# Building a causal filter's tap matrices with products on TensorE instead of a trip through DRAM

## The chip, the cores and the metric

The kernel runs on one core of a Trainium2 chip. The time is that of the whole device execution in microseconds, median of three runs. The engines are TensorE (PE in the profile; PEld is its weight load), VectorE (DVE), ScalarE (ACT), GpSimd (POOL) and SyncE (SP), which issues most of the transfers.

## What is computed

A causal filter of seven taps over the sequence, with softmax-normalised taps for each of 8 heads, and behind it two layers that expand 192 to 2048 and contract again, each with its own nonlinearity.

```python
# x: (2, 4096, 192), weight: (8, 7); a head has 24 of the 192 columns
w = exp(weight - max(weight)); w = w / (sum(w) + 1e-9)
out = einsum('hk,bskhg->bshg', w, windows_of_7(x_pad))     # filter over s
h = out.reshape(8192, 192) @ w_in                          # (192, 2048)
x = (h * clip(h + 3, 0, 6) / 6) @ w_out                    # layer 1
h = x @ w_in2
P = a[0] + a[1]*h + a[2]*h**2 + a[3]*h**3
Q = 1 + abs(b[0])*abs(h) + abs(b[1])*h**2
return (P / (Q + 1e-6)) @ w_out2                           # layer 2
```

## The kernel before

The 8192 rows are cut into 16 blocks of 512 (the last in two halves). Weights and activations are float32, split into a high and a low part; a product with weights runs three times (high by high, low by high, high by low). The contraction is laid out over 64 partitions, so that two products, one on partitions 0 to 63 and one on 64 to 127, run side by side on PE. The text calls these the two strands, L and H.

**The filter.** For each head a 64 x 128 matrix, `band`, holds the seven taps on shifted diagonals, and the filter is a product of `band` with the input rows. `band` has a copy on either half of the partitions. `xn` holds a block's rows as ten overlapping segments of 64 rows with 58 outputs each: five on partitions 0 to 63, five on 64 to 127. `conv0` and `conv1` (line 975 on) run the L and the H segments of four heads into one bank of PSUM; since both write the same bank, H starts only when L has ended (a *fence*, line 737: SP's queue is told by PE and tells PE). `conv_ev` copies the bank to SBUF (ACT, L1000), with a small copy on DVE (L998) that repeats the first heads at the row's end. `flip0`/`flip1` (L1012) then transpose with the reversing matrix `perm`, and ACT (L1024) and DVE (L1028) write the high and the low part into `X`, from which layer 1 reads. Blocks 0 and 1 are done ahead of all else and use the two banks `pre0` and `pre1`, which later are layer 1's accumulators; the first product of layer 1's contraction waits for block 1's last low part (`x1l2`).

**Making `band`.** `band_ops` (line 773) turns the taps, 7 numbers on 8 partitions, into the softmax with 19 small DVE instructions and transposes the result; `clear_line` and `store_line` write it into a zeroed DRAM line, `load_band` reads the line back with a stride of one element from partition to partition (twice, from SP and ACT), and `band_copy` copies it into `band` on ACT, POOL and DVE.

**Weights.** The 32 tiles of weights come as two words of 32 bits for each number and are put together on chip: `mag_w` on ACT (L869), `bound_w` on POOL or DVE (L874), three steps `bits_w` on DVE (L885, L888, L892), the high part on ACT (L903, L905), the low part on DVE or POOL (L912). A tile's raw words sit in one of four buffers; the next load into a buffer waits for the third step, which reads it last. PE cannot start a tile of the layer before its weights stand.

**What sets the order.** All instructions are listed with a due time and a guessed duration; `Issue.order` plays the list engine by engine and so fixes each engine's order; the numbers in `P` (offsets of due times, how far ahead an engine may look) steer it. Within an engine everything runs in that order. `warm` puts products of zeros on PE while it would idle at the start.

**The end.** The last block's contraction runs on exact words, and `P["GP"]` and `P["PATT"]` say which of its element-wise steps are done by POOL.

Of the kernel before, what the change touches and what calls it, by code (L numbers as in the profile page):

```python
# [27 lines left out]
 'CONV2': -0.275,  # L28
 'PAT': [1, 2],
 'PAT0': [1, 2],  # L30
 'PATT': [1, 2, 2, 2, 2, 2, 2, 0],
 'W1P': [-3.102, -2.87],
 'W2P': [6.57, 5.937],
 'WARM': 22,
 'TH': 0.001,
 'DUP': 2600,
 'WPART': {'c0': 0.1524, 'v0': 0.0728, 'vs': 0.0281, 'h0': 0.1693, 'l0': 0.2823},
 'HEAD': 32.39,
 'TAIL': 202.05,
 'D10': 3,  # L40
 'NEXT': -1.2,
# [11 lines left out]
          'dec': 65.4661,  # L53
          'conv': -4.205,
          'out': -156.0893,
          'x2': -18.5457,
          'fill': 999947.6802,
          'conv0': 26.2603},
 'OFF': {'mm1': -0.0531,
         'mm3': -0.6613,  # L60
         'mm2L': 1.4626,
         'mm2H': 2.4455,
         'mm4H': 1.0382,
         'mm4L': 0.3677,
         'u': -6.4348,
         'g': -32.961,
         'hi1': 4.7085,
         'lo1': -76.5356,
         'A': 3.8338,
         't1': 3.4597,  # L70
         'sq': 3.6846,
         'S': -175.4688,
         'q1': -55.5172,
         'q2': -103.6162,
         'q': -73.6019,
         't2': 3.5597,
         't3': -124.0539,
         'R': 4.9985,
         'RR': 5.6438,
         'w': -4.9954,  # L80
         'p2': -29.8916,
         'G': -111.7171,
         'hi2': 6.854,
         'lo2': 96.9644,
         'x2ah': -98.0086,
         'x2al': -54.7306,
         'x2mh': -3.2214,
         'x2ml': -14.6485,
         'x2mc': -67.402,
         'oa': -19.0233,  # L90
# [1254 lines left out]
```

## Time and profile before

| | us |
|---|---|
| three runs | 1232.18, 1232.56, 1233.94 |
| median | 1232.56 |
| profiled execution, its own time | 1232.17 |
| its span, first to last instruction | 1230.4 |
| PE busy | 1214.4 |
| DVE, ACT, POOL busy | 1137.3, 1140.7, 1107.9 |

The span is 1.8 us shorter than the execution that it belongs to. A busy PE is one with at least one product in flight; with two strands it can be busy and still do half of what it could. "Idle before" is an engine's idle time ahead of an instruction, and what stands behind the arrow released it.

### The profile page before, as it was taken

To read this page: it belongs to the slowest core of one execution; us is meant where nothing else is said; L and a number is where in the kernel's file an instruction comes from. 1 tells how busy PE (TensorE), PEld (TensorE's weight loads), DVE (VectorE), ACT (ScalarE), POOL (GpSimd) and SP (SyncE) were. 2 spreads that over 40 slices of the span, in tenths; PEclk is the share of its full clock that TensorE was granted. 3 is DMA by queue.
4 is the path that set the end of the run, shared out by engine and by line. 5 is a ranking of instruction groups with operands and counts; after the bars stand their busy time and mean duration, and the time that the engine had idled before them with its cause. 6 is when DMAs were issued, how large, how long until landed. Compare 5 with 4: busy or idle time off the path is not lost.

```text
span 1230.4 us, 31321 instructions
## 1 busy us (share of the span) xinstructions
PE 1214.4 (99%) x11334; PEld 1145.3 (93%) x11334; DVE 1137.3 (92%) x1807; ACT 1140.7 (93%) x2110; POOL 1107.9 (90%) x948
## 2 busy tenths in 40 slices
PE   9999999999999999999999999999999999999997
PEld 7788999899989999999999999999999999999997
DVE  6798999999999899899999999999999999999998
ACT  4677999999999999899999999999999999999996
POOL 3897998999989899898989989899899999999976
PEclk9999999999999999999999999999999999999999
DMA  6556003021030301203020020200202001011110
GB/s 161 142 161 157 18 2 71 2 52 21 1 71 2 72 1 25 48 2 72 1 52 21 11 63 2 54 19 14 59 14 50 10 15 44 14 28 27 52 28 14
DMA packets 75313, 51.46 MB, mean 42 GB/s; under 512 B 43290, under 2 KB 65174, under 8 KB 75158
## 3 DMA queue, kind: packets, MB, share of 16 engines
q1 hardware_dynamic: 74426, 48.89, 17.0%
q8 instruction: 89, 1.46, 0.5%
q10 hardware_dynamic: 732, 0.57, 0.2%
q14 instruction: 66, 0.54, 0.1%
HBM read 21.65 MB, written 7.87 MB: 24 GB/s over the span
## 4 chain that ended last, share of the span: by engine, by line
PE 84%; DVE 5%; ACT 5%; issue 2%; POOL 2%; DMA 1%; SPq 0%; DVEq 0%; ACTq 0%; POOLq 0%
PE acc L730 42%; PE bank L730 40%; PE warm L730 1%; DMA raw<-in_moe_w_out_dram 1%; DVE S L1192 1%; PE bank L1012 1%; DVE bank L1197 1%; DVE T L1165 1%; ACT T L1150 1%; ACT bank L1187 1%; ACT A L1146 1%; ACT A L1182 1%; DVE T L1205 1%; DVE T L1177 0%; POOL A L874 0%
## 5 line engine op out<-in xcount | busy, mean ns | idle before, releaser
L730 PE MATMUL bank<-X,Ih 64*128 64x512 f32 (+1 forms) x3264 | 905.6, 378 | 1.5 <-DVE T L1109 1.1
L730 PEld LDWEIGHTS bank<-X,Ih 64*128 64x128 f32 x3264 | 549.6, 184 | 20.6 <-DVE T L1109 1.9
L730 PE MATMUL bank<-X,Il 64*128 64x512 f32 (+1 forms) x1632 | 568.8, 375 | 0.0
L730 PE MATMUL acc<-g2h,O 64*128 64x512 f32 x1536 | 519.8, 392 | 2.1 <-SPq L737 2.0
L730 PE MATMUL acc<-g1h,O 64*128 64x512 f32 (+1 forms) x1536 | 493.7, 377 | 2.9 <-DVE X L1028 1.8
L730 PE MATMUL acc<-g2l,O 64*128 64x512 f32 x1024 | 397.0, 388 | 0.0
L730 PE MATMUL acc<-g1l,O 64*128 64x512 f32 (+1 forms) x1024 | 380.6, 374 | 0.3 <-POOL g1l L1117 0.3
L1171 POOL TENSOR_TENSOR S<-A,S 128x512 f32<-128x512 f32 x255 | 330.3, 1301 | 23.3 <-ACT A L1146 15.5
L1117 POOL TENSOR_TENSOR g1l<-u,g1h 128x512 fp32r<-128x512 f32 x240 | 311.9, 1300 | 31.1 <-ACT g1h L1113 25.6
L1220 POOL TENSOR_TENSOR g2l<-T,g2h 128x512 fp32r<-128x512 f32 x240 | 311.8, 1302 | 15.3 <-ACT g2h L1215 11.2
L730 PEld LDWEIGHTS bank<-X,Il 64*128 64x128 f32 x1632 | 290.8, 185 | 6.2
L730 PEld LDWEIGHTS acc<-g2h,O 64*128 64x128 f32 x1536 | 277.3, 184 | 11.7 <-SPq L737 4.8
L730 PEld LDWEIGHTS acc<-g1h,O 64*128 64x128 f32 x1536 | 276.3, 185 | 12.2 <-SPq L737 3.7
L1165 DVE SCALAR_TENSOR_TENSOR T<-T,coef,bank 128x512 f32<-128x512 f32 x256 | 190.2, 744 | 28.5 <-ACT A L1146 14.5
L1177 DVE SCALAR_TENSOR_TENSOR T<-T,coef,bank 128x512 f32<-128x512 f32 x256 | 190.4, 745 | 4.0 <-ACT A L1146 1.0
L730 PEld LDWEIGHTS acc<-g1l,O 64*128 64x128 f32 x1024 | 188.8, 184 | 5.1 <-POOL g1l L1117 0.7
L730 PEld LDWEIGHTS acc<-g2l,O 64*128 64x128 f32 x1024 | 188.5, 184 | 5.3
L1192 DVE SCALAR_TENSOR_TENSOR S<-S,bank 128x512 f32<-128x512 f32 x256 | 174.8, 683 | 13.5 <-ACT bank L1187 11.6
L1197 DVE SCALAR_TENSOR_TENSOR bank<-T,coef,bank 128x512 f32<-128x512 f32 x249 | 187.0, 751 | 0.0
L1150 ACT ACTIVATE T<-bank,coef 128x512 f32<-128x512 f32 x256 | 175.9, 688 | 10.2 <-PE bank L730 8.4
L1205 DVE SCALAR_TENSOR_TENSOR T<-S,bank 128x512 f32<-128x512 f32 x249 | 170.4, 684 | 4.1
L1109 DVE SCALAR_TENSOR_TENSOR u<-u,bank 128x512 f32<-128x512 f32 x240 | 163.5, 683 | 9.8 <-ACT u L1105 7.5
(104 smaller groups left out, 1797.5 us busy)
## 6 DMA issues: line engine op xcount, KB each, us to landing
X<-X SPq DMA_DIRECT2D x73, 256.0 KB, 3.3
raw<-in_moe_w_out_dram SPq DMA_DIRECT2D x16, 384.0 KB, 4.0
xn<-in_x_dram SPq DMA_DIRECT2D x27, 192.0 KB, 3.6
out_dram<-ov SPq DMA_DIRECT2D x60, 64.0 KB, 2.0
raw<-in_moe_w_in_dram SPq DMA_DIRECT2D x16, 192.0 KB, 3.7
raw<-in_moe_w_in_dram SPq DMA_DIRECT2D x16, 128.0 KB, 3.3
out_dram<-A SPq DMA_DIRECT2D x15, 128.0 KB, 2.0
saved<-A SPq DMA_DIRECT2D x8, 192.0 KB, 3.7
```

Of the source, the lines that this page charges most:

```text
L730: return nc.tensor.matmul(out=out, lhsT=lhsT, rhs=rhs, start=start, stop=stop, skip_group_check=True, **k)
L1012: i = nc.tensor.transpose(c[:, col:col + SPAN], src[:, 64 * part:64 * part + 128], rev[z])
L1109: stt(out=t, in0=t, scalar=1.0, in1=h1.pop((b, i)), op0=ALU.min, op1=ALU.mult)
L1117: nc.gpsimd.tensor_tensor(out=g1[b, i][1], in0=v1.pop((b, i)), in1=f32(g1[b, i][0]), op=ALU.subtract)
L1150: act(out=tile2(b, i, "T"), in_=h2[b, i], func=ACTF.Copy, scale=coef[:, 3:4])
L1165: stt(out=d["T"], in0=d["T"], scalar=coef[:, 2:3], in1=h2[b, i], op0=ALU.add, op1=ALU.mult)
L1171: (nc.gpsimd if k else nc.vector).tensor_tensor(out=d["S"], in0=d["A"], in1=d["S"], op=ALU.add if k == 1 else ALU.mult)
L1177: stt(out=d["T"], in0=d["T"], scalar=coef[:, 1:2], in1=h2[b, i], op0=ALU.add, op1=ALU.mult)
L1192: stt(out=d["S"], in0=d["S"], scalar=c1, in1=r2[b, i], op0=ALU.add, op1=ALU.mult)
L1197: stt(out=t if on_pool(b, i) else r2[b, i], in0=t, scalar=coef[:, 0:1], in1=r2[b, i], op0=ALU.add, op1=ALU.mult)
L1205: stt(out=d["T"], in0=d["S"], scalar=2.0, in1=k, op0=ALU.subtract, op1=ALU.mult)
L1220: nc.gpsimd.tensor_tensor(out=g2[b, i][1], in0=v2.pop((b, i))["T"], in1=f32(g2[b, i][0]), op=ALU.subtract)
```

## The change

**Taps.** `load_tap` reads the taps four times side by side (8 partitions x 28), and the same small DVE instructions run on them, without the transpose. A product with a small unit matrix (`band_rep`) spreads them over 128 partitions, one DVE product with a 0/1 mask (`band_diag`) keeps each head's tap where it belongs, and `band_mm` makes all bands in one PSUM bank with 16 float32 products of 32 columns, each of which is two passes on PE; behind each stands one pair of products of zeros. `band_ev` copies the bank into `band`, twice on ACT and twice on DVE. The 0/1 matrices are made at the start by POOL (one `iota`, four comparisons each for `step` and `eye`) and by DVE (`mask`). The DRAM line, its three transfers and `band_copy` are gone.

**Block 0.** Its L and H segments go into separate banks (`convz`): L into `pre0` and `pre1`, H into two ordinary banks, with no fence. `conv_ez` copies L on ACT, H on DVE, and the wrapped heads on DVE for each half.

**Order.** `P` has new numbers throughout. Fewer products of zeros stand at the start (5 rounds instead of 22). The loads of the first four weight tiles no longer wait for named events (`GATE`), the low part of the first weight tile moves from DVE to POOL (`LO0`), the convolution of block 2 is due earlier (`CONV2`), and in the last half block one `q` moves from DVE to POOL (`PATT`) and one product less runs on POOL (`GP`).

```diff
- 'CONV2': -0.275,
+ 'CONV2': -5.103,
- 'WARM': 22,
+ 'WARM': 5,
- 'PATT': [1, 2, 2, 2, 2, 2, 2, 0],
+ 'PATT': [1, 2, 2, 2, 2, 2, 2, 2],
- 'GATE': [2, 1, 2, 0],
+ 'GATE': [0, 0, 1, 0],
- 'LO0': [3],
+ 'LO0': [0, 3],
...
+        for hf in range(2 * (b == 0)):
+            for y in range(2):
+                k = ("pre", hf) if not y else ("bank", ("conv", hf))
+                at(t + hf * step, "c.trc", "LH"[y], 896, "convz", *(() if y else (4 + hf,)), hf, y, ...)
+                at(t + hf * step, "c.cv", "AV"[y], (451, 515)[y], "conv_ez", hf, y, ...)
...
-    at(-62, None, "S", 300, "store_line", ...)
-        at(-60 + 0.1 * z, None, "SA"[z], 480, "load_band", z, ...)
+    at(-64, None, "L", 300, "band_rep", r=[("line", 0), ("eye", 0)], w=[pb])
+    at(-63, None, "V", 90, "band_diag", r=[pb, ("mask", 0)], w=[("diag", 0)])
+    at(-62, None, "L", 16 * 180, "band_mm", r=[("diag", 0), ("step", 0)], w=[pb])
...
+    def ramp_of():
+        nc.gpsimd.iota(ramp.rearrange("p (a b) -> p a b", b=64), pattern=[[0, 3], [1, 64]], base=0, channel_multiplier=-1, ...)
+    def step_of(g):
+        r = slice(32 * g, 32 * g + 32)
+        nc.gpsimd.tensor_scalar(out=step[r], in0=ramp[r], scalar1=float(SPAN - 1 - 33 * g), scalar2=None, op0=ALU.is_equal)
+    def band_rep(home):
+        bandp[0] = bank[home]
+        mm(bandp[0][:, 0:4 * H], line, eye, True, True)
+    def band_diag():
+        nc.vector.tensor_tensor(out=diag, in0=bandp[0][:, 0:4 * H], in1=mask, op=ALU.mult)
+    def band_mm():
+        for q in range(16):
+            mm(bandp[0][:, 4 * H * q:4 * H * (q + 1)], step[:, 4 * q:4 * q + 128], diag, q == 0, q == 15)
+            warm(q + 200)
+            yield 180
+    def band_ev(half, z):
+        src = bandp[0].rearrange("p (j h) -> p h j", h=H)[row(z), half * HH:(half + 1) * HH]
+        dst = band[row(z), half * HH:(half + 1) * HH, 64 * z:64 * z + 64]
+        if z:
+            nc.vector.tensor_copy(out=dst, in_=src)
+        else:
+            act(out=dst, in_=src, func=ACTF.Copy)
...
+    def convz(home, half, z):
+        x1p["z", half, z] = home_of(home)
+        c = x1p["z", half, z][:, 0:HH * NS[0] * GC].rearrange("p (h s c) -> p h s c", h=HH, s=NS[0])
+        for h in range(HH):
+            h0 = half * HH + h
+            mm(c[:, h, 0:NS[z]], band[row(z), h0, :], xn[0][row(z), 0:NS[z], h0 * GC:(h0 + 1) * GC], h == 0, h == HH - 1)
+            yield 224
```

What the change makes of the order stands at three places. The first is SP's queue from the program's start. `raw` are weights, the first in-tile (three transfers), then the first out-tile (`in_moe_w_out`); `line_d` and `T` are the taps' trip. Before:

```order
L854 DMA raw_138<-in_moe_w_in_dram 64x3x256
L856 DMA raw_138<-in_moe_w_in_dram 64x2x256
L858 DMA raw_138<-in_moe_w_in_dram 64x256
L805 DMA line_d_123<-line1_114 7x8
L801 DMA T_112<-line_d_123 64x512
L1290 DMA perm_109<-in_ident_dram 128x320
L860 DMA raw_204<-in_moe_w_out_dram 128x2x384
L836 DMA coef_110<-in_moe2_a_dram 128x4
L854 DMA raw_214<-in_moe_w_in_dram 64x3x256
```

Now:

```order
L891 DMA raw_136<-in_moe_w_in_dram 64x3x256
L893 DMA raw_136<-in_moe_w_in_dram 64x2x256
L895 DMA raw_136<-in_moe_w_in_dram 64x256
L897 DMA raw_159<-in_moe_w_out_dram 128x2x384
L1346 DMA perm_109<-in_ident_dram 128x320
L891 DMA raw_187<-in_moe_w_in_dram 64x3x256
L893 DMA raw_187<-in_moe_w_in_dram 64x2x256
L895 DMA raw_187<-in_moe_w_in_dram 64x256
L897 DMA raw_227<-in_moe_w_out_dram 128x2x384
```

The first out-tile moved ahead of everything, and the second in-tile follows `perm` directly.

The second is DVE's queue from the first weight tile on. The rows that write `band` are the copies of the tap matrices; `A_266` before and `A_236` now are the first out-tile, `X_253` and `X_263` the filtered block 0. Before:

```order
L874 TENSOR_SCALAR bank0_105<-bank0_105 128x384
L885 TENSOR_SCALAR bank0_105<-bank0_105 128x384
L888 SCALAR_TENSOR_TENSOR bank0_105<-raw_138,bank0_105 128x384
L892 SCALAR_TENSOR_TENSOR bank0_105<-raw_138,bank0_105 128x384
L912 TENSOR_TENSOR Il0_128<-bank0_105,Ih0_127 128x384
L817 COPY band_111<-T_112 64x4x64 x2
L998 COPY X_253<-pre0_246 128x3x5x24
L885 TENSOR_SCALAR bank1_106<-A_266 128x384
L888 SCALAR_TENSOR_TENSOR bank1_106<-raw_204,bank1_106 128x384
L892 SCALAR_TENSOR_TENSOR A_266<-raw_204,bank1_106 128x384
```

Now:

```order
L911 TENSOR_SCALAR bank1_106<-bank1_106 128x384
L922 TENSOR_SCALAR bank1_106<-bank1_106 128x384
L925 SCALAR_TENSOR_TENSOR bank1_106<-raw_136,bank1_106 128x384
L929 SCALAR_TENSOR_TENSOR A_197<-raw_136,bank1_106 128x384
L922 TENSOR_SCALAR bank2_107<-A_236 128x384
L852 COPY band_111<-bank0_105 64x4x64 x2
L925 SCALAR_TENSOR_TENSOR bank2_107<-raw_159,bank2_107 128x384
L1037 COPY X_263<-pre0_290 64x3x5x24
L929 SCALAR_TENSOR_TENSOR A_236<-raw_159,bank2_107 128x384
L1037 COPY X_263<-bank3_108 64x3x4x24
L1037 COPY X_263<-bank3_108 64x4x4x24
L1037 COPY X_263<-bank1_106 64x4x4x24
```

The first step of the out-tile moved ahead of the band copies, the low part of the in-tile left DVE, and block 0 has four copies here where it had one.

The third is PE around the start of layer 1. `Ih`, `Il` are layer 1's weights, `pre` <- `X`,`band` is block 1's convolution. Before, the last of layer 1's first two tiles and then the convolution:

```order
L730 MATMUL bank0_105<-X_351,Il0_128 128x512
L730 MATMUL bank1_106<-X_351,Il0_128 128x512
L730 MATMUL bank0_105<-X_351,Ih0_127 128x512
L730 MATMUL bank1_106<-X_351,Ih0_127 128x512
L730 MATMUL pre1_255<-X_253,band_111 128x120 x4
L730 MATMUL pre0_246<-X_253,band_111 128x120 x2
L730 MATMUL pre1_255<-X_253,band_111 128x96
```

Now, behind the last zero product and ahead of layer 1, whose first product follows four rows later:

```order
L743 MATMUL warm1_145<-S_121 128x192
L743 MATMUL pre1_301<-X_263,band_111 128x120 x4
L743 MATMUL pre0_290<-X_263,band_111 128x120 x2
L743 MATMUL pre1_301<-X_263,band_111 128x96
L743 MATMUL pre0_290<-X_263,band_111 128x120
```

Block 1's convolution moved ahead of layer 1's first product.

## Rows read from the trace of the kernel before

**Rows 1.** page, part 1: busy us (share of the span) xinstructions
```profile
PE 1214.4 (99%) x11334; PEld 1145.3 (93%) x11334; DVE 1137.3 (92%) x1807; ACT 1140.7 (93%) x2110; POOL 1107.9 (90%) x948
```

**Rows 2.** table by stretch: stretch, length, busy of each engine, clock, DMA share, GB/s
```profile
5.00:10.00 5.00, 5.00 (x23) 2.58 (x23) 2.45 (x7) 0.52 (x1) 0.00 (x0) 1.00 0.29 62
...
10.00:15.00 5.00, 4.86 (x62) 4.50 (x59) 1.62 (x4) 1.77 (x3) 1.23 (x2) 1.00 0.99 249
...
60.00:80.00 20.00, 19.83 (x163) 17.05 (x164) 19.57 (x39) 16.56 (x33) 19.99 (x23) 1.00 0.56 158
...
120.00:1100.00 980.00, 977.48 (x8909) 931.95 (x8906) 916.32 (x1408) 943.94 (x1739) 908.20 (x763) 1.00 0.14 30
```

**Rows 3.** timeline, the taps: start us, us, engine, line, what [idle before <-releaser]
```profile
5.20 0.22 DVE L793 TENSOR_SCALAR line<-tmp,one 8x7 f32<-8x7 f32 x1
...
5.68 0.36 SPq L805 DMA_DIRECT2D line_d<-line  x1
...
11.20 0.72 ACT L815 ACTIVATE band<-T 64x256 f32<-64x256 f32 x1 [0.30 <-DMA T<-line_d]
...
12.26 0.70 DVE L817 COPY band<-T 64x256 f32<-64x256 f32 x2 [0.77 <-DMA T<-line_d]
```

**Rows 4.** timeline, weight loads of the warm products on PE
```profile
4.88 0.34 PEld L730 LDWEIGHTS warm<-S 128*128 128x128 f32 x1 [0.52 <-issue]
...
5.73 0.34 PEld L730 LDWEIGHTS warm<-S 128*128 128x128 f32 x1 [0.52 <-issue]
...
6.42 0.19 PEld L730 LDWEIGHTS warm<-S 128*128 128x128 f32 x1 [0.36 <-issue]
...
6.86 0.19 PEld L730 LDWEIGHTS warm<-S 128*128 128x128 f32 x1 [0.24 <-issue]
```

**Rows 5.** timeline, PE's weight loads in block 0's convolution
```profile
12.11 1.42 PEld L730 LDWEIGHTS pre<-xn,band 64*128 64x128 f32 x12
...
14.59 0.30 PEld L730 LDWEIGHTS pre<-xn,band 64*128 64x128 f32 x2
...
14.82 0.39 PEld L730 LDWEIGHTS warm<-S 64*128 64x128 f32 x4
...
15.04 0.30 PEld L730 LDWEIGHTS pre<-xn,band 64*128 64x128 f32 x2
```

**Rows 6.** timeline, the second weight tile: its load, ACT, then POOL
```profile
9.51 0.41 SPq L860 DMA_DIRECT2D raw<-in_moe_w_out_dram  x1
...
13.73 0.55 ACT L869 ACTIVATE A<-raw 128x384 f32<-128x384 f32 x1 [1.80 <-DMA raw<-in_moe_w_out_dram]
...
14.46 1.49 POOL L874 TENSOR_SCALAR A<-A 128x384 f32<-128x384 f32 x1 [2.54 <-ACT A L869]
```

**Rows 7.** timeline, ACT and DVE behind block 0's convolution
```profile
16.88 0.57 ACT L1000 ACTIVATE X<-pre 128x480 f32<-128x480 f32 x1 [1.22 <-PE pre L730]
...
15.70 0.53 DVE L998 COPY X<-pre 128x360 f32<-128x360 f32 x1 [2.74 <-ACT X L1000]
...
16.27 0.56 DVE L885 TENSOR_SCALAR bank<-A 128x384 int32<-128x384 int32 x1
```

**Rows 8.** timeline: PE, layer 1's tiles 1 and 3; DVE, block 1's last
```profile
20.90 0.41 PE L730 MATMUL bank<-X,Ih 64*128 64x512 f32 x1
...
25.82 0.50 PE L730 MATMUL bank<-X,Ih 64*128 64x512 f32 x1 [0.34 <-DVE u L1109]
...
33.77 0.69 DVE L1028 TENSOR_TENSOR X<-bank,X 128x512 fp32r<-128x512 f32 x1 [1.92 <-ACT X L1024]
```

**Rows 9.** chain of waits from 0 to 62 us: start us, us, what
```profile
37.75 8.25 DMA raw<-in_moe_w_out_dram
...
48.79 2.03 DMA raw<-in_moe_w_in_dram
...
52.62 5.34 DMA raw<-in_moe_w_out_dram
```

**Rows 10.** POOL's groups: xcount | busy us, mean ns | idle before
```profile
L1159 POOL TENSOR_SCALAR S<-A,coef 128x512 f32<-128x512 f32 x131 | 101.9, 778 | 23.8 <-ACT A L1146 14.7 <-DVE X L1131 3.3 <-PE acc L730 3.1
```

More of the change, by code (lines that the diff above doesn't have):

```diff
@@ L639, in make_plan @@
             z, step = "c." if first else "", 0.1 if first else 1.0
-        for hf in range(2):
+        for hf in range(2 * (b > 0)):
             tt = t + hf * step
@@ L648, in make_plan @@
             tt = t + (2 + hf) * step
-            key = transient(tt, pick(z, "trc"), "flip", 310, 248, b, hf, r=early + [("x1n0", b), ("x1n2", b) if hf == 2 else ("x1n1", b), ("perm", 0)] + [("x1n1", b)] * (hf == 2), kind="conv0" if first else "conv", early=5 * b + 2 + hf if first and hf < 2 else None)
+            key = transient(tt, pick(z, "trc"), "flip", 310, 248, b, hf, r=early + [("perm", 0)] + ([("x1n0", b), ("x1n1", b)] + [("x1n2", b)] * (hf == 2) if b else []), own=[("y", j) for j in range(2 + hf // 2)] * (not b), kind="conv0" if first else "conv", early=5 * b + 2 + hf if first and hf < 2 else None)
             xh, xl_ = (f"x1h{hf}", b), (f"x1l{hf}", b)
@@ L763, in warm @@
         k = kind % 2
-        if kind < 5:
+        if kind < 2:
             mm(spare[1], idle[:, 0:128], idle, True, True)
@@ L803, in store_line, with load_tap @@
-    def store_line():
-        ld = line_d[:]
-        nc.sync.dma_start(out=bass.AP(tensor=ld.tensor, offset=ld.offset + (SPAN - 1) * H, ap=[[H, KT], [1, H]]), in_=turn[0:KT, 0:H])
-    def clear_line():
-        ld = line_d[:]
-        nc.scalar.dma_start(out=bass.AP(tensor=ld.tensor, offset=ld.offset, ap=[[128, H], [1, 128]]), in_=zero)
-    def band_copy(e, half, z):
-        src = bandr.rearrange("p (j h) -> p h j", h=H)[row(z), half * HH:(half + 1) * HH]
+    def load_tap():
+        nc.scalar.dma_start(out=tap.rearrange("h (g k) -> h g k", g=4),
+                            in_=bass.AP(tensor=weight.tensor, offset=weight.offset, ap=[[KT, H], [0, 4], [1, KT]]))
@@ new lines, in eye_of @@
+    def eye_of():
+        for g in range(4):
+            nc.gpsimd.tensor_scalar(out=eye[:, g * H:(g + 1) * H], in0=ramp[0:H, 0:H], scalar1=0.0, scalar2=None, op0=ALU.is_equal)
+    bandp = {}
+    def band_rep(home):
[8 more added lines that the diff above has]
+            yield 180
@@ L1285, in conv_moe_moe_kernel @@
         act_table=lambda: nc.scalar.preload_act_table(ACTF.Abs_reciprocal_sqrt),
-        load_tap=lambda: nc.scalar.dma_start(out=tap, in_=weight),
-        zero_line=lambda: nc.vector.memset(zero, 0.0), zero_taps=lambda: nc.vector.memset(line, 0.0), clear_line=clear_line, zero_band=lambda z: nc.gpsimd.memset(band[row(z), :, 64 - 64 * z:128 - 64 * z], 0.0), band_copy=band_copy,
+        load_tap=load_tap,
+        zero_taps=lambda: nc.vector.memset(line, 0.0), zero_band=lambda z: nc.gpsimd.memset(band[row(z), :, 64 - 64 * z:128 - 64 * z], 0.0), ramp=ramp_of, step_of=step_of, mask_of=mask_of, eye_of=eye_of, band_rep=band_rep, band_diag=band_diag, band_mm=band_mm, band_ev=band_ev,
         band_op=lambda k: bops[k](),
-        store_line=store_line,
-        load_band=load_band, load_perm=lambda: nc.sync.dma_start(out=perm, in_=ident),
+        load_perm=lambda: nc.sync.dma_start(out=perm, in_=ident),
         load_coef=load_coef, coef_op=lambda k: cops[k](),
```

378 lines of the change are left out of this document (201 added, 177 removed), and 15 rows, old and new, of the table P.

## Prediction

> **What bounds the kernel now.** I read the busy line of the page first: PE 1214.4 of a span of 1230.4 us, the others 1108 to 1141 [rows 1]. Between 120 and 1100 us PE is busy 977.48 of 980 [rows 2], so nothing in the change can gain or lose much there unless it adds PE work. What it can move lies ahead of 120 us and in the last half block. Then the table by stretch: DMA carries 62 GB/s from 5 to 10 us and 249 GB/s from 10 to 15, when its engines are full (share 0.99) [rows 2]; the taps' trip and the weight load behind it sit in SP's queue in that order. Then the timeline of the head: the taps' line stands at 5.42, but ACT's first `band_copy` runs at 11.20 and DVE's last ends at 12.96 [rows 3], so PE's convolution begins at 12.11 [rows 5]. Layer 1 starts at 20.90 [rows 8] with two tiles, then pays for block 1's convolution, and its contraction waits for the low part that DVE starts at 33.77 [rows 8]. After that the chain of waits runs through weight loads: 8.25, 2.03 and 5.34 us of it [rows 9], each held back until DVE has read the buffer. So up to some 60 us DVE's progress in the weights sets the pace, and the wait that ends last is a load, not PE.
>
> **The bands.** The small DVE steps are the same in number but 28 columns wide instead of 7. The first price is hardly one of width (8x7 takes 0.22 at 5.20 [rows 3]), so I add 0.02 each for some 18: the line stands at about 5.75 instead of 5.42. `band_rep`, a hop to DVE for `band_diag` and a hop back I put at 0.9 together, an estimate of three steps like the 0.22 one with 0.1 between: `band_mm` starts at 6.7. On PE an instruction of so few columns costs its weight load. The like stands in block 0's convolution: the two loads of a product begin at 14.59, the four of two zero pairs at 14.82, the next product's at 15.04 [rows 5], so 0.23 for a product and 0.11 for a zero pair. A group of `band_mm` is one of each, 0.34; 16 of them are 5.4 us. Bounds: by an equal share of the 0.45 among the six loads, four are 0.30 and the whole 4.8; twelve loads of one product after another took 1.42 [rows 5], 0.12 each, and four loads at that price are 0.47, the whole 7.6. I take 0.34, since that stretch has the same two kinds in turn. End 12.1. ACT's two copies read 256 columns as `band_copy` did in 0.72 [rows 3], less if PSUM is read faster: the first L half stands at about 12.7, 0.8 later than before (11.92).
>
> DVE's two copies now stand behind the first step of the first out-tile. That tile's load was issued at 9.51 into a full queue, and ACT's step, which waited for it, began at 13.73 [rows 6]: 4.2 us. Now it stands fourth in SP's queue, at about 2.8 by the 0.4 to 0.7 an issue takes there; with the same 4.2 it is in at 7.0. The first in-tile and the input rows come in the same time, so I take 9.0. ACT's 0.55 and POOL's 1.49 [rows 6] bring it to 11.1, DVE's step of 0.56 [rows 7] to 11.7; then the bands are what is late, and with a hop and two copies of 0.35 [rows 3] DVE is done at 12.9, before 12.96. **Term A: +0.8** for the L half, 0 for the H half; +0.2 and -0.5 if a group takes 0.30, +3.0 and +2.2 if it takes 0.47.
>
> **Block 0's banks.** Before, ACT read the last product at 16.88, 4.77 after the first load at 12.11 [rows 5, 7]. Now four products of the first L half run alone (8 loads of 0.12, 0.95), the four of the second L half run beside the first H half in other banks (0.95 again, the two strands overlapping), and the four of the last H half have two zero pairs each, 0.45 [rows 5]: 3.7 in all. I take 0.8 of the 1.1, since ACT now reads two banks. **Term B: -0.8** (0 to -1.1), which pays for A: block 0's filter ends where it did. It costs four copies on DVE instead of one, 3 x 0.53 = 1.6 us [rows 7]; DVE stood idle for 2.74 ahead of that copy [rows 7], which hides them. Without that cover the 1.6 go onto the DVE term below.
>
> **Block 1's convolution ahead of layer 1.** Its eight products go in front of the first tile: side by side, four pairs at two loads of 0.12, about 1.0, of which PE idled or ran zeros for some part, so I put the first tile 0.6 later than 20.90, at 21.5. They no longer stand behind tile 2, so tile 3, at 25.82 and there 0.34 late on DVE's `u` [rows 8], comes 1.0 less 0.6 earlier, at about 25.4. **Term C: PE leads by 0.4.**
>
> **DVE's weights.** The wait of 1.92 that ended at 33.77 [rows 8] was for ACT's high part, hence for block 1's convolution on PE. Done before layer 1, that wait goes: the low part starts at 31.9. By the order four more steps of the weights, 0.56 each [rows 7], stand ahead of it, since the loads of the first tiles are no longer gated: 2.2 us. **Term D: DVE leads by about 4.0** (1.8 to 4.0). POOL takes over one low part of the first tile, in the time when it waited 2.54 for ACT [rows 6].
>
> **What reaches the end.** The three loads of the chain [rows 9] start when DVE's third step frees a buffer, so DVE's lead counts there and PE's alone doesn't. From 60 to 80 us POOL is busy 19.99 and DVE 19.57 of 20 [rows 2]; there a lead of PE is worth nothing unless DVE and POOL have it too, and POOL gains nothing but its earlier start. Between PE's 0.4 and DVE's 4.0 I take **-2.6**, nearer to DVE's since 15.6 us of the chain are loads. Terms A and B are the cause of C and are not added again.
>
> **Tail.** One `q` goes from DVE to POOL and one product back. A step of 512 columns is 0.69 on DVE [rows 8], on POOL 1.49 for 384 columns in one form [rows 6] and 0.78 for 512 in another [rows 10]. Each is 0.1 to 0.8 and they have opposite signs: 0, within 0.5. The middle, in another order with the same operations: 0, within 1, by PE's 977.48 of 980 [rows 2].
>
> **Sum.** The profiled execution took 1232.17, 1.8 of it outside the span; -2.6 gives 1229.6. The median lies 0.4 above that execution: **1230.0**, from 1228.6 with the whole of DVE's lead to 1232.2 with PE's alone.
>
> **Rivals.** *The head's lead is lost again* (R1): POOL at 19.99 of 20 [rows 2] is the bound from 50 to 120 and nothing of its work there is removed, so PE arrives sooner and waits more. For it: that row. Against it: the chain at 37 to 58 names loads, not POOL [rows 9]. Time 1232.4, no change that counts.
>
> *PE's clock falls back* (R2, slower). In the trace the weight loads of the same zero products come 0.85 apart until 5.73 and 0.44 from 6.42 on [rows 4]: PE worked at 1.2 GHz through products of zeros without a gap and was then raised to 2.4 (the mean clock of 1.00 for 5 to 10 us [rows 2] rounds the step away); every later stretch of that table has 1.00. Now only 5 rounds of zeros stand ahead of `band_rep`; at the spacing of [rows 4] they end near 5.3, and until 6.7 PE has little to do. If the clock is not raised before `band_mm`, its 5.4 us double: +5.4. If block 0's convolution runs low as well, 3.7 more: +9.1. It decides from 2.6 on, where the gain is used up. The time is then 1230.0 + 5.4 to 9.1, 1235.4 to 1239; I put 1237. Against it: the zero pair behind every product keeps PE occupied from 6.7 on. The Trainium skill, "TensorE: Matmul & The Clock Gate", Part 1, says that the throttled state is the default and that activity releases it; by that rule the start is slow in any case and the pairs behind the small passes count as activity. The trace agrees as to the start (0.85 against 0.44 [rows 4]); no run here shows a gap at that place.
>
> *POOL's constants come late* (R3). `iota` and eight comparisons must end before `band_rep` and `band_mm`. By a similar form, 0.78 for 512 columns [rows 10], 192 columns are 0.3 to 0.4, four of them 1.4, all done by 4 us. By the form of 1.49 for 384 [rows 6], 0.75 each, 3.0. POOL's first computing instruction of that kind came after idle time of 2.54 that ACT ended [rows 6], so any preparation of its code took at most that; both together put `step` at 7.5 to 8, and the bands up to 1.8 later: 1231.8. The Trainium skill, "GPSIMD Engine Reference", 2.1 Instruction dispatch, puts the first call of freshly loaded code at about 6 us; by an estimate from that page the bands come some 4.5 later and the sum ends near 1234.5. The trace disagrees here (2.54 at most).
>
> *More than DVE's lead* (R4): the waits between 40 and 60 go with the loads, and the whole 4.0 plus part of the 5.34 [rows 9] is saved: 1225.5 to 1228.
>
> **How the numbers follow.** Forecast 0.55, R1 0.20, R2 0.10, R3 0.07, R4 0.08. About 0.2%, 2.5 us, is what a measurement of this kernel can tell from no change; faster is below 1230.1. Half of the forecast lies below that, 0.29, and more of its weight towards DVE's lead, 0.33; with R4 and a little of R1 0.43. Slower, above 1235.0, is R2 and 0.02 for what I haven't named: 0.12. The rest, 0.45, is the same. The range of 8 in 10 leaves out R2, half of R4 and the upper end of R3: 1226.6 to 1233.6.
>
> **What would show it.** Right: in the timeline of the changed kernel `band_mm`'s groups 0.34 apart, ending at 12.1; DVE's band copies done by 12.9; layer 1's first tile at 21.5 and third at 25.4; block 1's last low part at about 30 to 32; fewer and shorter loads in the chain from 37 to 58. Wrong: load pitches of zeros of 0.85 after 6 us (R2); POOL's comparisons still running at 7 (R3); the third tile early but PE's idle time from 40 to 120 grown by as much (R1); or an operation of the middle in PE's way that the order moved, which I have priced at nothing.

## The result and the profile after

The changed kernel took 1241.75 us (median of 1241.75, 1244.49 and 1240.15) against 1232.56: a ratio of 1.0078, interval 1.0063 to 1.0093. It is slower by 9 us; the forecast was 1230.0. Its profiled execution has a span of 1240.0 us, 9.6 more than before. Of one run below (DRAM bands in the changed kernel's order) two of ten executions took 2060.97 and 1998.95 us at a mean granted clock of 0.635 and 0.556; its ratio leaves them out, its median of 1230.12 has them in and would be 1230.0 without them. The first part of the changed kernel's page, which answers to [rows 1]:

```profile
PE 1227.5 (99%) x11366; PEld 1148.9 (93%) x11366; DVE 1140.5 (92%) x1813; ACT 1138.3 (92%) x2110; POOL 1110.2 (90%) x957
```

PE is busy 13.1 us longer, the other engines within some 3 us of before. PE's idle time fell (12.5 us of the span against 16.0), so PE does something for longer and doesn't wait longer for the others. The table by stretch (columns as in [rows 2]) says where to look; the last line is the kernel before:

```profile
10.00:15.00 5.00, 5.00 (x21) 3.89 (x20) 0.56 (x1) 0.41 (x1) 1.57 (x2) 1.00 0.94 224
15.00:20.00 5.00, 5.00 (x21) 3.83 (x21) 0.00 (x0) 0.00 (x0) 0.00 (x0) 1.00 0.04 8
20.00:25.00 5.00, 5.00 (x24) 3.99 (x25) 0.00 (x0) 0.63 (x2) 0.00 (x0) 1.00 0.01 3
40.00:50.00 10.00, 9.58 (x79) 8.19 (x81) 9.86 (x20) 6.42 (x13) 7.85 (x7) 0.89 0.28 80
120.00:1100.00 980.00, 977.36 (x8885) 918.64 (x8885) 916.98 (x1409) 940.56 (x1735) 904.23 (x761) 1.00 0.14 30
...
15.00:20.00 5.00, 5.00 (x84) 5.00 (x85) 2.97 (x6) 2.91 (x6) 2.44 (x2) 1.00 0.90 223
```

From 120 to 1100 us PE is as busy as before (977.36 against 977.48), so the loss doesn't arise there. From 15 to 25 us DVE and POOL are idle throughout, DMA nearly so (share 0.04 and 0.01), and PE is "busy" 5.00 of 5.00 with 21 and 24 instructions, where the kernel before had 84 in 15 to 20, in and behind block 0's filter. The timeline of PE (start, us, what) shows with what:

```profile
6.77 0.60 PE L743 MATMUL bank<-u 8*128 8x32 f32 x2 [0.80 <-DVE u L806]
...
8.40 0.63 PE L743 MATMUL bank<-u,T 128*128 128x32 f32 x2
8.96 0.53 PE L743 MATMUL warm<-S 64*128 64x192 f32 x2
9.42 0.63 PE L743 MATMUL bank<-u,T 128*128 128x32 f32 x2
...
23.70 0.63 PE L743 MATMUL bank<-u,T 128*128 128x32 f32 x2
...
26.08 1.30 PE L743 MATMUL pre<-xn,band 64*128 64x120 f32 x5
...
36.90 0.47 PE L743 MATMUL bank<-X,Ih 64*128 64x512 f32 x1
...
47.02 0.72 PE L743 MATMUL acc<-g1h,O 64*128 64x512 f32 x2 [0.23 <-DVE X L1085]
```

`band_rep` runs at 6.77. Then come `band_mm`'s groups, two passes and a zero pair each, from 8.40 to 24.3: one group every 1.02 us (8.40, 9.42, ... 23.70), where the forecast had 0.34. Block 0's filter begins at 26.08, where its first weight load began at 12.11 before [rows 5], layer 1 at 36.90 instead of 20.90 [rows 8], and the first product of the contraction at 47.02 (31.44 before). ACT, DVE and POOL of the same stretch:

```profile
24.37 0.65 ACT L854 ACTIVATE band<-bank 64x256 f32<-64x256 f32 x2 [13.96 <-PE bank L743]
...
5.95 0.67 DVE L806 TENSOR_SCALAR u<-tmp,one 8x28 f32<-8x28 f32 x1
...
25.05 0.77 DVE L852 COPY band<-bank 64x256 f32<-64x256 f32 x2 [13.84 <-ACT band L854]
...
1.28 0.29 POOL L817 IOTA u<- 128x192 f32 x1
1.67 2.97 POOL L822 TENSOR_SCALAR T<-u 32x192 f32<-32x192 f32 x4
4.72 0.83 POOL L831 TENSOR_SCALAR u<-u 8x8 f32<-8x8 f32 x4
...
29.15 1.49 POOL L911 TENSOR_SCALAR A<-A 128x384 f32<-128x384 f32 x1 [17.58 <-ACT A L906]
```

DVE's two copies end at 25.82, 12.9 us after those of before [rows 3]. POOL's constants are no part of it: `iota` begins at 1.28, the four comparisons take 2.97 (0.74 each) and all is done by 5.55, ahead of the taps' line, which stands at 6.62. But POOL's next bound of a weight tile waits 17.58 us behind ACT, whose queue has the band copies first.

One thing in the table misleads: its clock column shows 1.00 from 10 to 25 us. The trace records clock grants only from the first change on. In the kernel before this first record is at 6.25 us, in the changed kernel at 30.76, with another loss from 47.82 to 51.24 (the 0.89 of the stretch 40 to 50). Ahead of the first record the column has 1.00 for want of one. That PE was at 1.2 GHz until 30.76 is read from the pitch, and the first experiment confirms the reading. The times of these records are counted from the start of the run's own span, as in the timelines; the recorded expectations below have some of them up to 0.1 us otherwise. Each is of the one execution that was profiled.

### The profile page after: what moved, and what is told of

Read it like the earlier page. It is cut to its first block, busy times and chain, and to the rows that moved or that the text cites. A ratio compares the mean times of both kernels' runs of the same rounds, so it can differ in the third digit from the quotient of the medians.

```text
span 1240.0 us, 31360 instructions
## 1 busy us (share of the span) xinstructions
PE 1227.5 (99%) x11366; PEld 1148.9 (93%) x11366; DVE 1140.5 (92%) x1813; ACT 1138.3 (92%) x2110; POOL 1110.2 (90%) x957
## 4 chain that ended last, share of the span: by engine, by line
PE 87%; DVE 7%; ACT 4%; issue 2%; POOL 0%; SPq 0%; DMA 0%; DVEq 0%; ACTq 0%
PE acc L743 43%; PE bank L743 41%; PE warm L743 1%; DVE S L1249 1%; DVE T L1222 1%; DVE bank L1254 1%; PE bank L1069 1%; DVE T L1262 1%; DVE T L1234 1%; ACT T L1207 1%; ACT A L1203 1%; ACT A L1239 0%; DVE u L1166 0%; ACT bank L1244 0%; PE pre L743 0%
## 5 line engine op out<-in xcount | busy, mean ns | idle before, releaser
L743 PE MATMUL bank<-X,Ih 64*128 64x512 f32 (+1 forms) x3264 | 891.0, 378 | 0.2 <-DVE T L1262 0.2
L743 PEld LDWEIGHTS bank<-X,Ih 64*128 64x128 f32 x3264 | 541.2, 185 | 21.3 <-DVE T L1262 1.6
L743 PEld LDWEIGHTS bank<-X,Il 64*128 64x128 f32 x1632 | 287.4, 185 | 7.5
L1222 DVE SCALAR_TENSOR_TENSOR T<-T,coef,bank 128x512 f32<-128x512 f32 x256 | 190.1, 745 | 29.6 <-ACT A L1203 12.5
```

Of the source, the lines that this page charges most:

```text
L743: return nc.tensor.matmul(out=out, lhsT=lhsT, rhs=rhs, start=start, stop=stop, skip_group_check=True, **k)
L1222: stt(out=d["T"], in0=d["T"], scalar=coef[:, 2:3], in1=h2[b, i], op0=ALU.add, op1=ALU.mult)
```

## The experiments

Theories at the start: the clock stays at 1.2 GHz through `band_mm` and more (the second rival of the prediction); the group of `band_mm` is dearer than forecast at either clock; the new order loses by itself.

**Full-height zeros at the start.** A full-height product uses all 128 partitions; a zero pair is two half-height products of 64 partitions, side by side. Here all five rounds are full-height, as the first five of the kernel before are:

```diff
-        if kind < 2:
+        if kind < 5:
             mm(spare[1], idle[:, 0:128], idle, True, True)
```

> The changed kernel with all five rounds of zeros at the start as full-height float32 products of 512 columns, like the first five rounds of the kernel before, instead of two such and three small pairs; nothing else differs, and the orders of the other engines stay. Theory 1 (clock): in the changed kernel the groups of band_mm come 1.02 us apart from 8.40 to 24.3 because PE stays at 1.2 GHz; the zeros now last until about 6.9, the clock rises near 6.3 as in the kernel before, the groups halve to about 0.51, DVE's band copies end near 17.5 instead of 25.8, and the time falls by 7 to 9 us to 1233 to 1235. Rival (price): the group costs 1.02 at either clock, since a full-height product and a half-height pair take turns; the time stays within 1 us of 1241.75. Rival (activity): the clock rises but falls again among the small passes: pitch 0.5 first, 1.0 later, time 1236 to 1240.

1240.96 us, ratio 1.0086 (1.0055 to 1.0116). The clock was granted at 7.43, and the timeline of PE has the price of a group at either clock, side by side:

```profile
9.77 0.41 PE L743 MATMUL bank<-u,T 128*128 128x32 f32 x2
10.11 0.36 PE L743 MATMUL warm<-S 64*128 64x192 f32 x2
10.40 0.41 PE L743 MATMUL bank<-u,T 128*128 128x32 f32 x2
...
15.12 0.63 PE L743 MATMUL bank<-u,T 128*128 128x32 f32 x2
15.68 0.53 PE L743 MATMUL warm<-S 64*128 64x192 f32 x2
16.14 0.63 PE L743 MATMUL bank<-u,T 128*128 128x32 f32 x2
```

0.63 us a group up to 14.2 (9.77 to 10.40), 1.02 from 15.12 on (to 16.14). The table by stretch of this run has the clock that goes with them:

```profile
10.00:15.00 5.00, 5.00 (x32) 3.88 (x31) 2.11 (x4) 0.52 (x1) 2.48 (x2) 0.93 0.91 229
15.00:20.00 5.00, 5.00 (x22) 3.87 (x20) 0.00 (x0) 0.00 (x0) 0.00 (x0) 0.50 0.12 25
```

So 1.02 is the group at 1.2 GHz, and at 2.4 GHz it is 0.63, not the 0.34 that I took from block 0's filter. Both first theories are right in part. And the grant didn't last: it was lost at 14.26, in the middle of `band_mm` with PE busy 5.00 of 5.00, and came back at 44.98 (lost again from 51.81 to 58.63). The activity rival had it right, with a time a little above its range. The profiled execution is the slowest of the four, 1247.94 us at a mean granted clock of 0.985; the others took 1240.28 to 1241.07 at 0.991 and 0.992, so their recorded losses are shorter.

**No zero pairs in `band_mm`.** Short start as in the changed kernel:

```diff
             mm(bandp[0][...], step[:, 4 * q:4 * q + 128], diag, q == 0, q == 15)
-            warm(q + 200)
```

> The changed kernel without the zero pairs behind band_mm's products; the rest, and the other engines' orders, stay. By the trace of the changed kernel the two passes take 0.56 of each 1.02 us. Theory 1 (clock): still 1.2 GHz, 16 x 0.56 = 9.0 us, band copies end near 19, 7 earlier; the time 1234 to 1237 if the clock rises in block 0's filter as it did. Rival (the pairs hold the clock): without them the low clock lasts through block 0's filter and on, so that less than half of the 7 us is kept: 1239 or more. Rival (full-height passes wait for their own ends): a group stays near 0.9 and little changes.

1240.08 us in one execution. The passes alone, on PE:

```profile
8.40 7.03 PE L743 MATMUL bank<-u,T 128*128 128x32 f32 x32
```

32 passes in 7.03, 0.44 a group at 1.2 GHz: the pair had cost 0.58 of the 1.02, not the 0.46 that the timeline suggests. That the changes between full-height passes and half-height pairs cost the rest is my reading; no run has pairs and passes of one height there. The bands were made 9 us earlier than in the changed kernel, and the time lies 1.7 below its median, inside its own 1240.15 to 1244.49: the first grant came at 37.34 instead of 30.76. That is the rival's case; where the nine microseconds went I put down to a filter and a start of layer 1 at half the clock.

**DRAM bands or TensorE bands by themselves, planned anew.** The band parts of the two kernels exchanged in the list of instructions, with the numbers in `P` kept. In the first the changed kernel has the trip through DRAM, in the second the kernel before has `band_mm`:

```diff
-    at(-62, None, "L", 16 * 180, "band_mm", ...)
+    at(-62, None, "S", 300, "store_line", ...)
+        at(-60 + 0.1 * z, None, "SA"[z], 480, "load_band", z, ...)
```

> The changed kernel with the bands made by the trip through DRAM and the zeros at the start as in the kernel before; block 0's separate banks and the new table of numbers stay. Theory 1 (clock in band_mm is the whole loss): the bands stand near 13 as before, and what is left is the gain that the forecast gave to the order and the banks, 1228 to 1232.5. Rival (order): the new table costs by itself, DVE's copies and a second low stretch of the clock at 48 to 52 us remain: 1236 or more.

> The kernel before with the bands made on TensorE as in the changed kernel, five full-height rounds of zeros at the start instead of 22 mixed ones; block 0's shared bank and the old table of numbers stay. Theory 1: the clock is high, band_mm costs 16 x 0.51 = 8.2 us, the bands stand near 17, 4 later than by the DRAM trip: 1235 to 1237. Rival (activity): the clock falls back in band_mm, bands near 25: 1241 or more. Rival (order): the bands are harmless and the loss comes from the table: 1231 to 1233.5.

1264.57 us (ratio 1.0274, 1.0238 to 1.031) and 1280.02 (1.0396, 1.0375 to 1.0417), far above the ranges of their first theories; by the letter the rivals "1236 or more" and "1241 or more" have them, but they say nothing about the parts. The planner plays all instructions with their guessed durations, so another list gives another order: of DVE's 1809 rows in the one, 1234 stand in the order of the changed kernel, of 1811 in the other, 1217 in that of the kernel before (longest common sequence of operations and shapes). In the first of the two the clock was lost six times after the first grant, up to 1242 us into the run. The numbers in `P` fit one list. From here on an edit was made in what a step emits, not in the list, so that the orders stay.

**A short start in the kernel before.** Its bands and all its orders, but the short start of zeros of the changed kernel:

```diff
-        if kind < 5:
+        if 5 <= kind < 22:
+            return
+        if kind < 2:
...
-                n = C if kind < 17 else 192
+                n = 192
```

> The kernel before with only the changed kernel's short start of zeros (two full-height products of 512 columns and three small pairs instead of 22 rounds); bands by the DRAM trip, every engine's order as before. It asks what a late clock alone costs. Theory 1 (a late clock is the loss): PE runs out of zeros near 6, its first grant of 2.4 GHz comes at 20 us or later instead of 6.25, and the time is 8 to 12 us above the kernel before, 1240 to 1245. Rival (the head is bound by loads and DVE, and PE's clock hardly matters there): within 3 us of the kernel before, 1231 to 1236, although the clock comes as late.

1238.02 us, ratio 1.0041 (1.0026 to 1.0056): 5.3 us for the short start and the late clock behind it, between the two expectations. The first grant came at 4.56, was lost at 7.97 while PE idled (it waited 5.78 for the bands), and returned at 28.45. The changed kernel begins with the same four full-height passes and had no grant before 30.76: what the start brings differs between executions. PE's filter and first tile, then the table:

```profile
11.74 3.74 PE L730 MATMUL pre<-xn,band 64*128 64x120 f32 x22 [5.78 <-ACT band L817]
...
26.34 0.68 PE L730 MATMUL bank<-X,Ih 64*128 64x512 f32 x1
```

```profile
5.00:10.00 5.00, 0.95 (x16) 0.78 (x15) 2.79 (x7) 0.62 (x2) 0.00 (x0) 0.80 0.34 73
...
20.00:25.00 5.00, 5.00 (x58) 5.00 (x58) 1.49 (x3) 2.50 (x6) 1.49 (x1) 0.50 0.26 67
```

The first tile runs at 26.34 instead of 20.90, 5.4 later, and the span of this execution, the fastest of the four, is 1234.1 instead of 1230.4: 3.7 of the 5.4 arrive at the end.

**DRAM bands in the changed kernel's order.** The same exchange as above, but inside the steps: `band_diag` does the transpose and issues the trip, `band_rep`, `band_mm` and the 0/1 matrices emit nothing, the start has the 22 rounds. 1802 of DVE's 1809 rows stand in the order of the changed kernel. Addresses are shortened to `<line_d>`, and the lines of the start are left out.

```diff
     def band_diag():
-        nc.vector.tensor_tensor(out=diag, in0=bandp[0][:, 0:4 * H], in1=mask, op=ALU.mult)
+        nc.vector.transpose(out=turn, in_=lin)
+        nc.sync.dma_start(out=<line_d>, in_=turn[0:KT, 0:H])
+        <nc.sync, nc.scalar>.dma_start(out=bandr[row(z)], in_=<line_d>)
```

> The changed kernel with its orders, its separate banks for block 0 and its table kept as they are, but the bands made by the trip through DRAM and the 22 rounds of zeros of the kernel before, written in at the places of the steps that they replace. Theory 1 (band_mm and the short start lose the clock, and the rest of the change is sound): first grant near 6.5 us and no loss of it before 60 us, bands at 13, time 1227.5 to 1232.5, as the forecast's terms for order and banks have it. Rival (the new order loses the clock by itself at the start of layer 1, as the changed kernel did from 47.9 to 51.3 us): a low stretch between 30 and 60 us remains and the time is 1234 to 1240.

1230.12 us, ratio 0.9986 (0.997 to 1.0002): 11.6 below the changed kernel with the same orders and the same separate banks. So order and banks cost nothing, and the bands on TensorE with their short start are the whole loss. A gain over the kernel before isn't shown, as the interval reaches above 1. The grant came at 6.40. The rival was also right in one point: it was lost from 33.71 to 40.53. PE's start of filter, first tile and contraction, then the store of the taps' line, the band copies on ACT and DVE, and block 1's last low part:

```profile
14.31 0.79 PE L743 MATMUL pre<-xn,band 64*128 64x120 f32 x5 [1.21 <-POOL A L926]
...
23.69 0.48 PE L743 MATMUL bank<-X,Ih 64*128 64x512 f32 x1
...
33.81 1.22 PE L743 MATMUL acc<-g1h,O 64*128 64x512 f32 x2 [0.22 <-DVE X L1100]
```

```profile
7.42 0.36 SPq L855 DMA_DIRECT2D line_d<-u  x1
...
13.54 1.22 ACT L869 ACTIVATE band<-T 64x256 f32<-64x256 f32 x2 [1.30 <-DMA T<-line_d]
...
14.14 0.87 DVE L867 COPY band<-T 64x256 f32<-64x256 f32 x2
...
34.14 0.68 DVE L1100 TENSOR_TENSOR X<-bank,X 128x512 fp32r<-128x512 f32 x1
```

The table by stretch of this run, and then the last two stretches of the kernel before:

```profile
30.00:35.00 5.00, 4.67 (x41) 3.83 (x40) 5.00 (x11) 3.79 (x8) 4.59 (x6) 0.87 0.37 91
35.00:40.00 5.00, 5.00 (x27) 4.70 (x27) 2.54 (x6) 1.39 (x3) 1.84 (x2) 0.50 0.28 84
40.00:60.00 20.00, 19.96 (x175) 17.32 (x174) 17.69 (x34) 15.94 (x31) 17.57 (x18) 0.99 0.69 186
60.00:120.00 60.00, 59.97 (x532) 53.52 (x529) 54.99 (x103) 47.15 (x92) 53.88 (x54) 1.00 0.53 149
```

```profile
40.00:60.00 20.00, 18.28 (x159) 15.34 (x158) 15.88 (x30) 14.88 (x30) 18.02 (x16) 1.00 0.58 157
60.00:120.00 60.00, 59.58 (x498) 50.84 (x499) 56.26 (x106) 46.70 (x91) 54.53 (x54) 1.00 0.56 152
```

and its first contraction product on PE:

```profile
31.44 0.50 PE L730 MATMUL acc<-g1h,O 64*128 64x512 f32 x1 [1.80 <-DVE X L1028]
```

Until 40 us this run is no better than before: the contraction starts at 33.81 (31.44 before) and block 1's last low part at 34.14, against 33.77 [rows 8]. Then PE's waits of 1.72 between 40 and 60 us are gone (19.96 of 20 against 18.28), and from 60 to 120 PE does 532 instructions instead of 498. The chain of waits, in which [rows 9] had 15.6 us of weight loads from 37 to 58, holds none from 20 to 80 us, and from 33.81 on it is PE's own work, which begins with this piece:

```profile
33.81 2.50 PE acc L743 x5
```

**Five full-height rounds and no pairs.** Both first edits together, bands on TensorE:

> The changed kernel with the five full-height rounds of zeros at the start and without the zero pairs in band_mm. In the run with the five rounds alone the clock was granted at 7.5 us, a group took 0.63 then, and it was lost again at 14.3 in the middle of band_mm, until 45.0. Theory 1 (the stretch of small passes loses the clock): without pairs the 16 groups take 16 x 0.22 = 3.5 us at 2.4 GHz and end near 13.5, before the clock would go; it then stays through block 0's filter and the time is 1230 to 1235. Rival (small passes lose it whatever their number, and the pairs had helped): lost at about 14 again, first layer at 1.2 GHz, 1240 or more.

1230.28 us, ratio 0.999 (0.9974 to 1.0006), 11.5 below the changed kernel with `band_mm` kept. The passes on PE, and the table:

```profile
8.99 3.76 PE L743 MATMUL bank<-u,T 128*128 128x32 f32 x32
```

```profile
10.00:15.00 5.00, 5.00 (x43) 4.96 (x43) 2.78 (x6) 1.51 (x4) 2.46 (x2) 0.77 0.95 228
15.00:20.00 5.00, 5.00 (x53) 5.00 (x53) 1.96 (x5) 2.42 (x5) 2.01 (x2) 0.55 0.35 91
35.00:40.00 5.00, 4.78 (x27) 4.31 (x27) 3.63 (x7) 2.24 (x6) 2.51 (x4) 0.66 0.44 133
```

16 groups in 3.76, 0.23 each, done at 12.75. The grant was at 5.86; it was lost at 12.68, returned at 19.51, and was lost from 36.58 to 39.99. So ending the passes before 14 us did not keep the clock, as the theory had it, but the two losses together last 10.2 us, where the changed kernel was low for some 30. Put beside the first two runs: the longer start alone gained 0.8 us and leaving out the pairs alone 1.7, both together 11.5.

**Wider zero pairs.** The run with five rounds, its pairs widened from 192 to 512 columns:

> The changed kernel with the five full-height rounds at the start and the zero pairs in band_mm widened from 192 to 512 columns. Theory 1 (what holds the clock is how much PE streams): groups of about 0.34 + 0.42 = 0.76 us, no loss at 14.3, bands near 22.5, and the time 1235 to 1239, below the 1240.96 of the narrow pairs although band_mm is longer. Rival (the full-height passes or the change between them and the pairs lose the clock, whatever the pairs' width): lost before 20 us, 1243 or more.

1244.17 us, ratio 1.0092 (1.0072 to 1.0112). Granted at 4.47, lost at 14.71, returned at 31.78, lost from 48.85 to 52.26: the loss in `band_mm` stays, and longer groups are paid on top. The rival's number. Pairs between the passes, narrow or wide, did not hold the clock.

**Narrow zeros without data.** The run with DRAM bands in the changed kernel's order, plus 16 full-height float32 products of zeros, 32 columns wide, in `band_mm`'s place:

```diff
         for q in range(16):
+            mm(spare[q % 2][:, 0:32], idle[:, 0:128], idle[:, 0:32], True, True)
             yield 180
```

> The run with the changed kernel's orders, the bands by the DRAM trip and the long start of zeros (1230.12 us, clock granted from 6.34 to 33.65 us), with one thing added: at band_mm's place 16 full-height float32 products of zeros, 32 columns wide, which nobody waits for and which run while the bands are still on their way. Theory 1 (a stretch of narrow full-height passes alone loses the clock): a loss before 20 us and a time of 1232 to 1238. Rival (it takes the waits on data, or the later filter, to lose it): no loss before 30 us and 1229 to 1231.

1237.0 us, ratio 1.003 (1.0013 to 1.0048), 6.9 above the same run without them. The table:

```profile
10.00:15.00 5.00, 5.00 (x55) 4.66 (x53) 1.22 (x4) 2.19 (x4) 2.46 (x2) 1.00 0.54 145
15.00:20.00 5.00, 5.00 (x50) 4.96 (x50) 1.25 (x4) 1.00 (x2) 0.01 (x1) 0.67 0.70 171
20.00:25.00 5.00, 5.00 (x56) 5.00 (x55) 3.49 (x8) 1.41 (x3) 4.08 (x4) 0.50 0.25 81
```

Granted at 6.45, lost at 16.69, until 37.17, and again from 43.99 to 50.82. The narrow passes run from 12.26 to 16.02. Nobody waits for their results, and they do no arithmetic on data. With the zero pairs behind them they keep PE until 16.9, so that the filter starts 2.6 later (16.91 against 14.31); the rest, 4.3 by the medians and 2.8 by the two ratios, I put down to the clock. The seven executions bear that out: they take 1231.94 us at a mean granted clock of 0.996 up to 1240.25, the profiled one, at 0.989, where the run without the zeros has seven at 0.997 or 0.998 and one at 0.990. That 32 narrow full-height passes lead to the loss is shown; how much of them it takes is not.

**A denser start.** Four full-height rounds, wide pairs ahead of and behind `band_mm` and one in its middle, no pairs behind the products:

> The changed kernel, bands on TensorE, with the start made dense: four full-height rounds of zeros and one wide pair, no pairs behind band_mm's products but one wide pair in their middle, and wide pairs ahead of and behind band_mm; the other engines' orders stay. The run with five rounds and no pairs lost the clock from 12.63 to 19.46 and took 1230.28. Theory 1 (narrow passes without dense ones between lose it): granted near 6, no loss before 30 us, bands near 13, and 1227 to 1229.5, below both kernels. Rival (any band_mm loses it): lost between 11 and 16 again, 1230 to 1235.

1232.1 us, ratio 1.0011 (0.9993 to 1.0028). Granted at 6.85, lost from 13.68 to 20.50 and from 37.57 to 44.40. Dense work around `band_mm` doesn't prevent the loss either; the time is 1.8 above the plain run, with intervals that overlap. A miss for the theory as I had put it.

**Wide pairs in block 1's transposes and block 2's filter,** where the second loss follows; first with DRAM bands, then with bands on TensorE:

```diff
             x1p["f", b, part][1] = i
+            if b == 1 and k == 2:
+                warm(300 + z)
...
             x1p["c", b, half][1] = i
+            if b == 2 and h % 2:
+                warm(300 + z)
```

> The run with the changed kernel's orders, DRAM bands and the long start (1230.12 us; clock lost from 33.65 to 40.47, behind block 1's narrow transposes and block 2's filter), with a zero pair of 512 columns behind the third product of each of block 1's transposes and behind every second product of block 2's filter; nothing else is changed. Theory 1 (stretches of narrow products lose the clock, dense ones between keep it): no loss before 60 us; 14 pairs of 0.21 cost at most 3 us of PE, some of it where it waited; time 1226 to 1229.5. Rival (the loss there has another cause, such as the waits for data): still lost between 30 and 40 and 1230.5 to 1234.

> The run with bands on TensorE without pairs and with five full-height rounds of zeros (1230.28 us; clock lost from 12.63 to 19.46 and from 36.53 to 39.94), with the same wide pairs in block 1's transposes and block 2's filter. Theory 1: the second loss goes, the first stays; 1228 to 1230. Rival (as above): both losses stay and the pairs cost 1 to 3 us, 1231 to 1234.

1229.87 us (ratio 0.9991, 0.9976 to 1.0005) and 1229.97 (0.9985, 0.9971 to 0.9998). The table of the second:

```profile
10.00:15.00 5.00, 5.00 (x43) 4.96 (x43) 2.73 (x6) 1.17 (x3) 1.88 (x2) 0.76 0.99 227
30.00:35.00 5.00, 5.00 (x56) 4.43 (x54) 4.52 (x10) 3.31 (x7) 4.01 (x3) 1.00 0.00 0
35.00:40.00 5.00, 4.93 (x48) 4.41 (x49) 4.31 (x8) 3.11 (x8) 2.64 (x3) 1.00 0.54 161
```

In both profiled executions the loss between 33 and 40 us is gone (0.66 had stood for 35 to 40 in the run without the pairs, here 1.00). In the first another came instead, from 20.12 to 30.36, which its companion without the pairs had not had; the first loss of the second, from 12.58 to 19.41, stayed as expected. Where a loss falls differs between executions, so one profile doesn't prove it. The mean granted clock of all twelve executions of the first says more: five are at 1.000 and took 1228.65 to 1229.56, two are at 0.993 and took 1235.51 and 1236.31. In the run without the wide pairs none was above 0.998. So the same program varies by some 7 us with the clock alone, and the wide pairs let some executions through without a loss, though the median of 1229.87 is no better. The second is the only version here whose interval lies below the kernel before: bands on TensorE, five full-height rounds, no pairs in `band_mm`, wide pairs in the transposes. Its upper end is 0.9998 and many versions were tried, so the gain of some 2.8 us is weakly shown.

## Why the prediction was wrong

- **The bands.** This step failed, in two terms. The group was priced at 0.34 from block 0's filter, where products and pairs are both half-height; full-height passes and half-height pairs take turns at 0.63 at 2.4 GHz, 4.6 us more for 16. And 2.4 GHz was assumed: 1.02 against 0.63 is 6.2 more. 5.4 + 4.6 + 6.2 make 16.2, measured 15.9 from 8.40 to 24.3. A measured upper bound of 0.47 a group was too low, because none of the rows showed the two kinds mixed. Against it stands a plain 0.23 without the pairs.
- **The clock.** The second rival named the mechanism, and I gave it 0.10 and 1235.4 to 1239; the 1241.75 lie above that, in part since it doubled a group of 0.34. The argument against it was the mistake: that the pairs behind every product keep PE at work. I also took the clock column's 1.00 for 5 to 10 us for a rounded step, when it has no record ahead of 6.25. With pairs, wide pairs, no pairs or nothing but narrow zeros, the grant was lost in or right behind the narrow passes, with PE busy 5.00 of 5.00. And PE stayed low through most of block 0's filter, to 30.76: its first five products took 1.30, where they take 0.79 in the run with DRAM bands. The Trainium skill, "TensorE: Matmul & The Clock Gate", Part 1, says that activity releases the throttle. The traces agree in part: the grant came at 6.25 behind the long start and at 30.76 behind the short one, but at 4.56 with the short start in the kernel before. What they add is that a PE that the profile calls busy without a gap was at 1.2 GHz from 8.40 to 30.76.
- **The taps' line** came at 6.62, not 5.75: the last step began 0.75 later than in [rows 3] (5.95 against 5.20), where I had 0.33, and took 0.67 instead of 0.22. Its output is strided now; that this is the reason isn't tested. `band_rep` with its two hops took 1.78 (6.62 to 8.40) instead of 0.9. Both together are the rest of the bands' delay: `band_mm` began 1.7 later than forecast.
- **POOL's constants** (third rival): not late. The dear form was right, 0.74 a comparison, and `iota` began 0.04 us behind the memset. The 6 us that the Trainium skill, "GPSIMD Engine Reference", 2.1 Instruction dispatch, has for the first call of freshly loaded code don't show here.
- **Block 0's banks and block 1's convolution ahead of layer 1.** With DRAM bands in the changed kernel's order the first tile comes 9.4 us behind the filter's start (14.31 to 23.69), 8.8 before (12.11 to 20.90), with block 1's filter now ahead of it: the forecast had 0.6 for that, and it is 0.6. But its first tile as a whole is 2.8 later than before, since the trip through DRAM came later in this run: the line is stored at 7.42 (5.68 before [rows 3]), ACT's copy waits for the load until 13.54, where it ran at 11.20, and DVE's copies end at 15.01. So the run doesn't show when the forecast's bands would have stood.
- **DVE's lead** of 4.0 was not there: block 1's last low part runs at 34.14, as before. Waits and weight loads after 40 us are gone from the chain all the same, and order and banks alone give 1230.12 where the forecast said 1230.0. That agreement is luck: no lead reached 40 us, the interval doesn't part the 1230.12 from the kernel before, and what gain there is comes behind 40 us, where I had put the new order at nothing.
- **R1**, that a lead is lost again from 50 to 120 us, wasn't put to the test: in no run did the head lead. Against it speaks that in the run with DRAM bands POOL is at 20.00 of 20 in 60 to 80 too, and PE does more there than before. In the changed kernel POOL is busy 60.00 of 60 from 60 to 120 (54.53 before), which may limit what is caught up; that isn't tested. Part of a delay at the start is given back: 16.0 us at the first tile of the changed kernel are 9.6 at the end of its span, 5.4 in the short-start run are 3.7.

## What to carry to other kernels

Before small products are moved onto TensorE, ask at which clock they will run and what the work behind them will pay if they lose it: here 16 us of narrow passes ran at half the clock, and most of the filter behind them did too. Price a mixed stretch only from a stretch with the same mix of heights, and leave out filler whose use isn't shown: here it raised a group from 0.23 to 0.63 at 2.4 GHz and the clock was lost all the same. Look at the granted clock of every execution and not of the profiled one alone. An experiment on one part of a planned kernel has to keep the plan; put it into what a step emits, and count the rows whose order stayed.

## What the runs showed of the hardware

- PE lost the 2.4 GHz grant while it was busy without a gap: at 14.26 between narrow full-height passes and pairs, at 12.68 in plain narrow passes, at 16.69 behind narrow zeros. It also lost it while idle (7.97, in the short-start run), but the wait of 1.80 ahead of 31.44 in the kernel before lost nothing in the profiled execution, whose mean clock is 1.000; its other executions go down to 0.995.
- The clock column shows 1.00 ahead of the first recorded grant, while the pitch of the groups (1.02 against 0.63) shows 1.2 GHz. Pitch of equal work is the safer reading at a program's start.
- A full-height pass and a half-height pair taking turns cost 0.63 a group at 2.4 GHz, the full-height part alone 0.23.
- Executions of one program differ in where and how long they are at 1.2 GHz, and their time follows: 1228.65 to 1229.56 us at a mean clock of 1.000, 1235.51 and 1236.31 at 0.993, in the run with DRAM bands and wide pairs.
- Which property of the narrow passes loses the grant, and why the second loss near the start of the contraction comes and goes, stays open.
